# Recurrent attention and a squared-ReLU layer on one core: other load shapes, v through GpSimd's casting queue, state by head pairs, and priorities written out

## The chip, the cores and the metric

The kernel runs on one core of one Trainium2 chip. The metric is the device time of one execution in microseconds, as the median of several runs. Engines are called by the names that the profile uses: PE (TensorE matmuls), PEld (TensorE weight loads), DVE (VectorE), ACT (ScalarE), POOL (GpSimd), SP (SyncE, which issues most DMAs).

## The reference

Inputs are r, k and v of shape (4, 8, 768, 48), that is 4 batches, 8 heads, 768 steps and 48 columns, w and u of shape (8, 48), and two weight matrices of 384 x 2048 and 2048 x 384, all float32.

```python
for t in range(S):
    kt, vt, rt = (k[:, :, t].copy(), v[:, :, t].copy(), r[:, :, t].copy())
    cur = np.einsum('bhd,bhe->bhde', u[None] * kt, vt)
    y[:, :, t] = np.einsum('bhd,bhde->bhe', rt, state + cur)
    state = w[None, :, :, None] * state + np.einsum('bhd,bhe->bhde', kt, vt)
...
h = x @ w_in                 # x: y with the heads of a token side by side, (3072, 384)
r = np.maximum(h, 0.0)
return (r * r @ w_out).astype(np.float32)
```

## The kernel before

**Units.** The 768 steps are cut into 6 chunks of 128. A unit is one chunk of one batch, all heads: 24 units, unit i being chunk i // 4 of batch i % 4. In a unit the recurrence becomes matmuls. r is multiplied by w to the power (t - 64) (`wpos`) and k by w to the power (63 - t) (`wneg`), both by `scale` on DVE (L321), into a padded bfloat16 tile `rkw`. It is transposed to `rkT`, for units 0 to 5 by PE (`turn` L341, evicted by ACT, L345), and from unit 6 on by a DMA (`turn_dma` L330). Then come `at` (L358, r times k for all pairs of steps), `mask` (DVE, L370), `rk` (DVE, L350) and `sums` (L378 for the u term, L383 for the unit's part of the state), `diag_v` (`dv`, DVE, L392), `y_mm` (L421, and L427 with the state of the chunk before), and `evict_y` (`yb`, DVE, L436). The state is kept in float32 as (128, 4, 48): partitions 0 to 63 hold the even head of a pair and 64 to 127 the odd one. `state_add` (L400, L402) and `state_cast` (L412) therefore run twice, on 64 partitions each, and `state_decay` (L406) once. v is loaded as float32 and cast by ACT (`cast_v`, L325).

**The layer.** `yb` is transposed into `xT`, for units 0 to 5 by PE (L452, evicted by ACT, L456) and later by a DMA (L445). `mm1` (L468) makes a block of 512 columns of h in one PSUM bank: 12 matmuls for one unit, or 6 with both units of a pair (units 8 to 19 go in pairs). ACT applies ReLU (L476), and the square is made by ACT (L483) or DVE (L485) after the pattern `SQUARES`. `mm2` (L492) accumulates 16 matmuls a unit in quarters of four, ACT evicts (L499), and SP stores. The last unit is stored in two parts (L508 to L520).

**Weights.** The two matrices come in four pieces each, `w_in_q0` to `w_in_q3` and `w_out_q0` to `w_out_q3`, cast to bfloat16 by GpSimd's DMA queue. Each piece is held back by a small copy (L306) that reads one load of the table `FRONT`, so that it is issued only when that load has landed.

**Order.** Nothing is scheduled at run time. `Plan.run` takes all steps with an engine, a cost, what they need, the buffers and banks they take, and a rank. It plays them through in time: each engine takes the first step by rank that is ready, and PE is given matmuls on a constant tile (`fill`, L276) while it would be idle in the first 16 us. The instructions are then written out per engine in that order, and each engine works through its own list strictly in order, waiting where an operand is not there. A DMA in the plan has a cost on its queue and a transfer of its own; SP's transfers pass in the order of issue.

**Start.** `wrow` (L222) is w broadcast to 128 partitions by one DMA on ACT's queue. ACT takes its logarithm (`lnw`, L241) and the two exponentials `wpos` and `wneg` (L245). `wu` (w and u again) comes by GpSimd's queue, is transposed by PE (L281), copied by DVE (L284), and makes `uwb` (POOL, L287 and L290) and `wend`, w to the power 128 (ACT, L293 and L294).

Of the kernel before, what the change touches and what calls it, by code (L numbers as in the profile page):

```python
# [16 lines left out]
class Plan:  # L17
# [9 lines left out]
    def __init__(self, lags, cold, spare):  # L27
        self.lags = lags
        self.cold = cold
        self.spare = spare  # L30
        self.steps = []
        self.at = {}
        self.users = {}
        self.place = {}

    def add(self, key, engine, cost, emit, needs=(), rank=0.0, new=(), uses=(), move=None):
        s = dict(key=key, engine=engine, cost=cost, emit=emit, rank=rank, new=new, move=move)
        s["needs"] = [n for n in needs if n is not None]
        self.at[key] = s
        self.steps.append(s)  # L40
        for x in tuple(new) + tuple(uses):
            self.users.setdefault(x, []).append(s)

    def run(self, room, banks, count):
# [10 lines left out]
        begin, until, tight, loose = self.spare  # L55
        held[0] = "spare"
# [7 lines left out]
        def ready(s, e):  # L64
            if s["move"]:
                return s["end"] + moved
# [96 lines left out]
def kernel(  # L163
# [23 lines left out]
    NPAD = 5  # L187
    SQUARES = 'AMAMAAAM'
    FRONT = (
        ("I", 0, ("kt", 1)), ("I", 1, ("kt", 3)), ("I", 2, ("kt", 3)), ("O", 0, ("kt", 3)),  # L190
        ("I", 3, ("kt", 3)), ("O", 1, ("kt", 3)), ("O", 2, ("kt", 3)), ("O", 3, ("kt", 3)),
# [5 lines left out]
    loads = ctx.enter_context(tc.tile_pool(name="loads", bufs=6))  # L197
# [6 lines left out]
    plan = Plan((0.9, 0.0, 0.2, 0.33, 0.12), (5.5, 1.9), (1.25, 16.0, 0.057, 0.08))  # L204
# [16 lines left out]
    wrow = const.tile([128, dm], F32)  # L221
    nc.scalar.dma_start(out=wrow, in_=w.rearrange("h d -> (h d)").unsqueeze(0).to_broadcast([128, dm]))  # L222
    nc.scalar.preload_act_table_set("natural_log_exp_and_others")
    warm = const.tile([128, 128], BF16)
    nc.vector.memset(warm, 1.0)  # L225
    wu = const.tile([HP, 2, 2, 64], F32)
# [3 lines left out]
    nc.gpsimd.dma_start(out=wu[:, 1, :, :D], in_=u.rearrange("(p o) d -> p o d", o=2))  # L230

    iota_i = const.tile([128, 1], mybir.dt.int32)
    nc.gpsimd.iota(iota_i, pattern=[[0, 1]], base=0, channel_multiplier=1)
    up = const.tile([128, 1], F32)
    nc.vector.tensor_scalar(up, iota_i, 1.0, -float(C // 2), ALU.mult, ALU.add)
    down = const.tile([128, 1], F32)
    nc.vector.tensor_scalar(down, iota_i, -1.0, float(C // 2 - 1), ALU.mult, ALU.add)
    ident4 = const.tile([HP, HP], F32)
    make_identity(nc, ident4)
    lnw = const.tile([128, dm], F32)  # L240
    nc.scalar.activation(lnw, wrow, AF.Ln)  # L241
    wpos = const.tile([128, H, D], F32)
    wneg = const.tile([128, H, D], F32)
    for wx, by in ((wpos, up), (wneg, down)):
        nc.scalar.activation(wx.rearrange("p h d -> p (h d)"), lnw, AF.Exp, scale=by)  # L245
# [15 lines left out]
    st32 = [const.tile([128, HP, D], F32, name=f"st32_{b}") for b in range(B)]  # L261
    stb = [const.tile([128, HP, 2 * D], BF16, name=f"stb_{b}") for b in range(B)]
    for b in range(B):
        nc.vector.memset(stb[b], 0.0)

    wend_c = const.tile([128, HP], F32)
    wend = wend_c.unsqueeze(2).to_broadcast([128, HP, D])
# [7 lines left out]
    def fill():  # L275
        nc.tensor.matmul(out=banks[0][:, :128], lhsT=warm, rhs=warm, start=True, stop=True)  # L276

# [17 lines left out]

    def load(i, name):
        c, b = units[i]
        src = {"rt": r, "kt": k, "vt": v}[name]
        x = loads.tile([C, H, D], F32, name=name)
        nc.sync.dma_start(  # L300
            out=x, in_=src[b, :, c * C : (c + 1) * C, :].rearrange("h s d -> s h d")
        )
# [14 lines left out]
    def scale(i, x):  # L317
        t = tiles[i]
        t["rkw"] = rkw_b[i % NPAD]
        src, wx = (t["kt"], wneg) if x else (t["rt"], wpos)  # L320
        nc.vector.tensor_tensor(t["rkw"][:, x, :, :, :D], pair(src), pair(wx), ALU.mult)  # L321

    def cast_v(i):
        tiles[i]["vb"] = work.tile([C, H, D], BF16, name="vb")
        nc.scalar.copy(tiles[i]["vb"], tiles[i]["vt"])  # L325

    def turn_dma(i):
        t = tiles[i]
        t["rkT"] = work.tile([128, 2, HP, C], BF16, name="rkT")
# [5 lines left out]
    def turn(i, x):  # L335
        t = tiles[i]
        t["tp", x] = bank("h", i, "rk", x).bitcast(BF16)[:, : HP * C].rearrange("p (a c) -> p a c", a=HP)
        if x == 0:
            t["rkT"] = work.tile([128, 2, HP, C], BF16, name="rkT")
# [3 lines left out]
    def evict_rk(i, x):  # L343
        t = tiles[i]
        nc.scalar.copy(t["rkT"][:, x], t["tp", x])  # L345
# [48 lines left out]
    def state_add(i):  # L394
        c, b = units[i]
        for o in range(2):
            sl = slice(o * 64, o * 64 + 64)
            x = tiles[i]["s"][sl, :, o * D : (o + 1) * D]
            if c == 0:
                nc.vector.tensor_tensor(st32[b][sl], x, wend[sl], ALU.mult)  # L400
            else:
                nc.vector.tensor_tensor(st32[b][sl], x, st32[b][sl], ALU.add)  # L402
# [5 lines left out]
    def state_cast(i):  # L408
        b = units[i][1]
        for o in range(2):  # L410
            sl = slice(o * 64, o * 64 + 64)
            nc.scalar.copy(stb[b][sl, :, o * D : (o + 1) * D], st32[b][sl])  # L412
# [127 lines left out]

    add("w", ACT, 3.9, None, rank=-1e3)
    add("wk", ACT, 0.48, None, rank=-1e3, needs=["w"])
    copy("begin", SP, 0.74, None, rank=-1e3)
    add("wu", POOL, 4.6, None, rank=-1e3)
# [3 lines left out]
    add("wend", ACT, 0.4, end_columns, rank=10, needs=["copied"])  # L548
    for n, (what, q, gated) in enumerate(FRONT):
        copy(  # L550
            (what, q), POOL, 1.0, do(weights, gated, q, what), rank=n,
            move=((2.35, 98, 1.25, 0.0) if what == "I" else (2.05, 78, 1.25, 0.0)), needs=[gated], uses=[gated],
        )
    for i in range(NU):
# [4 lines left out]
        for n, name in enumerate(("rt", "kt", "vt")):  # L559
            copy(  # L560
                (name, i), SP, 0.55, do(load, i, name), rank=rank + 0.1 * n, move=(1.06, 16, 0.67, 1.0),
                new=[(name, i)],
            )
        for x in range(2):
            add(
                ("scale", i, x), DVE, 0.47, do(scale, i, x), rank=a - 4 + 0.1 * x,
                needs=[("rt", i) if x == 0 else ("kt", i), "wk" if x else "w", ("scale", i - 1, x) if i else None],
                new=[("rkw", i)] if x == 0 else (), uses=[(("rt", "kt")[x], i), ("rkw", i)],
            )
        add(  # L570
            ("vb", i), ACT, 0.405, do(cast_v, i), rank=a + 0.5, needs=[("vt", i), ("rkT", i) if i < 24 else ("scale", i, 1)],
# [142 lines left out]
```

## Time and profile before

| | |
|---|---|
| median of 3 runs | 178.01 us (177.97 to 179.85) |
| the profiled execution | 179.7 us, of which the span from the first to the last instruction 177.9 |
| PE busy | 167.5 us (94%), 2080 matmuls |
| DVE, ACT busy | 128.7 and 128.8 us (72% each) |
| POOL busy | 11.4 us (6%) |
| DMA | 29.05 MB in 107,385 packets, 101,985 of them under 512 bytes |
| granted clock | 1.0 |

The page shows one execution. The busy shares say which engine was occupied, not which one the others waited for; that is told by the waits and by the chain that ended last. The slices are 177.9 / 40 = 4.45 us each, one digit being tenths of a slice. "Packets" are runs of contiguous bytes: a load of r, k or v for one unit is 192 KB in 1,024 runs of 192 bytes (48 float32 of one head and step). A line such as `L402 ... x32 | 11.3, 352 | 0.2` reads: 32 instructions, 11.3 us busy, 352 ns each, 0.2 us of idle time of that engine just before them.

### The profile page before, as it was taken

The page shows a single profiled execution, that of the slowest core. Times are in us where ns is not written, and L with a number is a line of the kernel's source. Part 1 is how long each engine was busy: PE and PEld are TensorE (multiplying, and loading weights), DVE is VectorE, ACT ScalarE, POOL GpSimd, SP SyncE. Part 2 cuts the span into 40 slices and gives each one's busy share as a digit, 9 for nine tenths or more (in the row PEclk, how much of TensorE's full clock was granted, in tenths as well). Part 3 has the DMA queues.
Part 4 walks back from the last instruction along what each step waited for, and adds up shares of the span by engine and source line. Part 5 has one row for each costly group of instructions (what it writes and reads, how often), then busy time and mean ns, then how long its engine had stood idle before and what let it go on. Part 6 is the DMA issues. An engine that isn't in the chain of part 4 may idle for free.

```text
span 177.9 us, 5106 instructions
## 1 busy us (share of the span) xinstructions
PE 167.5 (94%) x2080; PEld 135.2 (76%) x2080; DVE 128.7 (72%) x279; ACT 128.8 (72%) x268; POOL 11.4 (6%) x35
## 2 busy tenths in 40 slices
PE   7699689999999999989979999899999999999993
PEld 7599479977786886876776796786795797878762
DVE  3389996565989899769779698589598695853100
ACT  2738889999385985597488599488597499659820
POOL 7120950000000000000000000000000000000000
PEclk9999999999999999999999999999999999999999
DMA  5999999999797888869879889999998897940212
GB/s 103 192 179 181 163 197 197 208 190 179 93 208 128 169 155 171 175 132 206 174 161 185 176 166 191 133 201 185 163 199 172 187 201 135 314 135 0 71 67 90
DMA packets 107385, 29.05 MB, mean 163 GB/s; under 512 B 101985, under 2 KB 106849, under 8 KB 107361
## 3 DMA queue, kind: packets, MB, share of 16 engines
q1 hardware_dynamic: 104976, 25.37, 75.1%
q0 software_dynamic: 2240, 3.15, 10.0%
q8 instruction: 16, 0.26, 0.6%
q10 hardware_dynamic: 144, 0.20, 0.6%
q14 instruction: 9, 0.07, 0.1%
HBM read 20.65 MB, written 4.72 MB: 143 GB/s over the span
## 4 chain that ended last, share of the span: by engine, by line
PE 57%; DMA 18%; DVE 17%; issue 3%; ACT 2%; SPq 1%; ACTq 0%
PE bank L492 22%; PE bank L468 22%; DMA rkT<-rkw 8%; DMA rt<-in_r_dram 5%; DVE am L370 4%; DVE rkw L321 4%; DVE yb L436 3%; PE bank L358 3%; DMA xT<-yb 2%; PE bank L276 2%; DMA wrow<-in_w_dram 2%; DVE dv L392 2%; DVE g L485 2%; PE bank L421 1%; PE bank L508 1%
## 5 line engine op out<-in xcount | busy, mean ns | idle before, releaser
L468 PE MATMUL bank<-xT,w_in_q 128*128 128x128 bf16 (+1 forms) x864 | 71.8, 237 | 0.5 <-ACT xT L456 0.3
L476 ACT ACTIVATE gr<-bank 128x512 f32<-128x512 f32 x96 | 55.0, 601 | 19.5 <-PE bank L468 18.9
L468 PEld LDWEIGHTS <-w_in_q 128*128 128x128 bf16 x864 | 64.4, 114 | 3.3 <-issue 0.7
L492 PE MATMUL bank<-w_out_q,g 128*128 128x384 bf16 x368 | 65.1, 326 | 0.0
L492 PEld LDWEIGHTS <-g 128*128 128x128 bf16 x368 | 34.4, 98 | 20.0
L370 DVE TENSOR_TENSOR am<-bank,smask 128x512 bf16<-128x512 f32 x48 | 31.8, 684 | 8.2 <-PE bank L358 8.1
L483 ACT ACTIVATE g<-gr 128x512 bf16<-128x512 f32 x60 | 37.3, 639 | 0.6
L485 DVE TENSOR_TENSOR g<-gr 128x512 bf16<-128x512 f32 x36 | 24.6, 687 | 13.1 <-ACT gr L476 13.0
L499 ACT COPY osb<-bank 128x384 f32<-128x384 f32 x23 | 11.0, 484 | 10.1 <-PE bank L492 7.9
L412 ACT CAST stb<-st 64x192 bf16<-64x192 f32 x40 | 14.0, 350 | 5.1 <-DVE st L406 4.4
L350 DVE TENSOR_TENSOR rk<-rkT 128x512 bf16<-128x512 bf16 x24 | 10.1, 422 | 7.7 <-DMA rkT<-rkw 5.6
L321 DVE TENSOR_TENSOR rkw<-rt,wpos 128x384 bf16<-128x384 f32 x24 | 13.2, 552 | 2.5 <-DMA rt<-in_r_dram 1.7
L436 DVE TENSOR_TENSOR yb<-bank,dv 128x384 bf16<-128x384 f32 x24 | 13.3, 555 | 2.3 <-PE bank L427 1.7
L392 DVE TENSOR_TENSOR dv<-vb,bank 128x384 f32<-128x384 bf16 x24 | 13.1, 545 | 2.6 <-PE bank L383 2.6
L321 DVE TENSOR_TENSOR rkw<-kt,wneg 128x384 bf16<-128x384 f32 x24 | 13.2, 551 | 0.6 <-DMA kt<-in_k_dram 0.3
L276 PE MATMUL bank<-warm 128*128 128x128 bf16 x108 | 11.9, 275 | 1.1 <-DVE warm L225 1.1
L358 PE MATMUL bank<-rkT 64*128 64x128 bf16 x192 | 9.8, 222 | 2.8 <-DMA rkT<-rkw 1.9
L325 ACT CAST vb<-vt 128x384 bf16<-128x384 f32 x24 | 12.2, 508 | 0.2
L402 DVE TENSOR_TENSOR st<-bank,st 64x192 f32<-64x192 f32 x32 | 11.3, 352 | 0.2
L358 PEld LDWEIGHTS <-rkT 64*128 64x128 bf16 x192 | 5.5, 96 | 7.5 <-issue 2.9
L276 PEld LDWEIGHTS <-warm 128*128 128x128 bf16 x108 | 9.6, 128 | 1.4 <-DVE warm L225 1.1
L345 ACT COPY rkT<-bank 128x512 bf16<-128x512 bf16 x12 | 6.9, 585 | 4.5 <-PE bank L341 4.5
(54 smaller groups left out, 97.8 us busy)
## 6 DMA issues: line engine op xcount, KB each, us to landing
rt<-in_r_dram SPq DMA_DIRECT2D x24, 192.0 KB, 4.2
kt<-in_k_dram SPq DMA_DIRECT2D x24, 192.0 KB, 4.0
vt<-in_v_dram SPq DMA_DIRECT2D x24, 192.0 KB, 4.4
out_dram<-osb SPq DMA_DIRECT2D x23, 192.0 KB, 2.8
w_in_q<-in_moe_w_in_dram POOLq DMA_DIRECT2D x4, 384.0 KB, 7.2
w_out_q<-in_moe_w_out_dram POOLq DMA_DIRECT2D x4, 384.0 KB, 13.1
rkT<-rkw SPq DMA_TRANSPOSE x18, 3.8
xT<-yb SPq DMA_TRANSPOSE x18, 3.0
```

The source lines that it names most:

```text
L276: nc.tensor.matmul(out=banks[0][:, :128], lhsT=warm, rhs=warm, start=True, stop=True)
L321: nc.vector.tensor_tensor(t["rkw"][:, x, :, :, :D], pair(src), pair(wx), ALU.mult)
L358: nc.tensor.matmul(out=t["at"][o][:, p, :], lhsT=t["rkT"][sl, 1, p, :], rhs=t["rkT"][sl, 0, p, :], start=True, stop=True,)
L370: nc.vector.tensor_tensor(am, t["at"][o], smask.unsqueeze(1).to_broadcast([C, HP, C]), ALU.mult)
L392: nc.vector.tensor_tensor(t["dv"], t["vb"], t["d"].unsqueeze(2).to_broadcast([C, H, D]), ALU.mult)
L412: nc.scalar.copy(stb[b][sl, :, o * D : (o + 1) * D], st32[b][sl])
L436: nc.vector.tensor_tensor(t["yb"], t["y"], t["dv"].rearrange("p h d -> p (h d)"), ALU.add)
L468: nc.tensor.matmul(out=t["h", s][:, a], lhsT=turned, rhs=chunks[c]["xT"][:, n, b : b + m, :], start=(n == 0), stop=(n == NK - 1),)
L476: nc.scalar.activation(t["gr", s], t["h", s], AF.Relu)
L483: nc.scalar.activation(g, x, AF.Square)
L485: nc.vector.tensor_tensor(g, x, x, ALU.mult)
L492: nc.tensor.matmul(out=t["o"], lhsT=chunks[units[i][0]]["g"][:, f, units[i][1], :], rhs=w_out_q[f // 4][:, f % 4, :], start=(f == 0), stop ...
```

## The change

1. w is loaded as one row on one partition. ACT takes the logarithm there, and PE spreads it: `spread_log` by four float32 matmuls with a row of ones, 32 partitions for each pair of heads, and `spread_all` by one to all 128. `power_r` (four exponentials), `power_k` and `power_rest` make `wpos`, `wneg` and `wnat`.
2. r of units 0 to 5 is loaded with a pair of heads and 32 groups of four steps on the partitions, so that one run is four steps, 768 bytes; two DMAs for one. `scale` reads it in that layout, the transposes take one step of each group of four, and `evict_rk` puts the columns back in order as it copies. From unit 6 on r is loaded as before and multiplied by `wnat`.
3. v of units 6 to 23 is loaded by GpSimd's queue, cast to bfloat16 on the way, into 8 buffers of their own (`load_v`). They stand last in GpSimd's list, after all weights, and no `cast_v` is left for them. For the plan each of them needs kt of the unit before; as an instruction it waits for its buffer alone.
4. The state is (128, 4, 96): both heads of a pair in all partitions, with a zero in `wend` for the cross terms. `state_add` and `state_cast` are one instruction each.
5. A table `TURNS` gives single steps a rank of their own; `FRONT` gates w_in_q1 by kt of unit 2 (it was unit 3), w_in_q2 by vt of unit 1, and the pieces of w_out and w_in_q3 by kt3, kt4, rt4 and vt4; `SQUARES` gives six of eight squares to ACT, not five; `rkw` has 8 buffers for 5, loads 7 for 6, `rkT` and `vb` 6 for 4; some costs in the plan are others.

On PE's list the fillers go from 108 to 87. On DVE's list yb of unit 0 stands behind the scaling of r of unit 2, the masks of unit 5 behind the scaling of k of unit 7, and yb of unit 5 behind rk of unit 6. SP's list begins rt0, kt0, rt1, vt0, kt1, kt2, vt1, vt2, rt2, rt3, kt3, kt4, vt3, rt4, vt4, rt5, rt6, vt5, kt5, kt6, rt7, kt7, rt8, and then the first transpose, rkT of unit 6. GpSimd's list has w_in_q0, w_in_q1, `wend`, w_in_q2, w_out_q0, w_out_q1, w_in_q3, w_out_q2, w_out_q3, and then the 18 loads of v.

```diff
     def add(self, key, engine, cost, emit, needs=(), rank=0.0, new=(), uses=(), move=None):
+        kind, which = (key[0], key[1] if len(key) == 2 else key[1:]) if isinstance(key, tuple) else ("", key)
+        rank = self.turns.get(kind, {}).get(which, rank)
...
-    NPAD = 5
-    SQUARES = 'AMAMAAAM'
+    NPAD = 8
+    NVB = 8
+    SQUARES = 'AAAMAAAM'
+    TURNS = {
+        "rt": {
+            0: -42.651, 1: -34.809, 11: 17.689, 12: 18.622, 14: 29.051, 16: 41.802, 18: 45.897, 2: -17.657, 21:
...
-        ("I", 0, ("kt", 1)), ("I", 1, ("kt", 3)), ("I", 2, ("kt", 3)), ("O", 0, ("kt", 3)),
-        ("I", 3, ("kt", 3)), ("O", 1, ("kt", 3)), ("O", 2, ("kt", 3)), ("O", 3, ("kt", 3)),
+        ("I", 0, ("kt", 1)), ("I", 1, ("kt", 2)), ("I", 2, ("vt", 1)), ("O", 0, ("kt", 3)),
+        ("O", 1, ("kt", 4)), ("O", 2, ("rt", 4)), ("O", 3, ("vt", 4)), ("I", 3, ("kt", 4)),
...
-    wrow = const.tile([128, dm], F32)
-    nc.scalar.dma_start(out=wrow, in_=w.rearrange("h d -> (h d)").unsqueeze(0).to_broadcast([128, dm]))
+    wrow = const.tile([1, dm], F32)
+    nc.scalar.dma_start(out=wrow, in_=w.rearrange("h d -> (h d)").unsqueeze(0))
...
+    def spread_log():
+        spread["r"] = bank("h", "rlog")[:, : 2 * D]
+        for a in range(HP):
+            sl = slice(a * 32, a * 32 + 32)
+            nc.tensor.matmul(
+                out=spread["r"][sl], lhsT=ones[:, :32], rhs=lnw[:, a * 2 * D : (a + 1) * 2 * D], start=True, stop=True,
+            )
+
+    def spread_all():
+        spread["k"] = bank("h", "klog")[:, :dm]
+        nc.tensor.matmul(out=spread["k"], lhsT=ones, rhs=lnw, start=True, stop=True)
+
+    def power_r():
+        for l in range(4):
+            nc.scalar.activation(wpos[:, l].rearrange("p o d -> p (o d)"), spread["r"], AF.Exp, scale=up[:, l : l + 1])
...
-        nc.sync.dma_start(
-            out=x, in_=src[b, :, c * C : (c + 1) * C, :].rearrange("h s d -> s h d")
-        )
+        if name == "rt" and i < NPE:
+            src = src.rearrange("(a o) (q l) d -> o a q (l d)", o=2, l=4)
+            for o in range(2):
+                nc.sync.dma_start(out=x[:, o * 4 : o * 4 + 4, :].rearrange("p l d -> p (l d)"), in_=src[o])
+        else:
+            nc.sync.dma_start(out=x, in_=src.rearrange("h s d -> s h d"))
...
+    def load_v(i):
+        c, b = units[i]
+        tiles[i]["vb"] = work.tile([C, H, D], BF16, name="vc", bufs=NVB)
+        nc.gpsimd.dma_start(out=tiles[i]["vb"], in_=v[b, :, c * C : (c + 1) * C, :].rearrange("h s d -> s h d"))
...
+            turned = t["tp", 0].rearrange("p l (a q) -> p a l q", a=HP)
+            nc.scalar.copy(t["rkT"][:, 0].rearrange("p a (q l) -> p a l q", l=4), turned)
...
-        for o in range(2):
-            sl = slice(o * 64, o * 64 + 64)
-            x = tiles[i]["s"][sl, :, o * D : (o + 1) * D]
-            if c == 0:
-                nc.vector.tensor_tensor(st32[b][sl], x, wend[sl], ALU.mult)
-            else:
-                nc.vector.tensor_tensor(st32[b][sl], x, st32[b][sl], ALU.add)
+        nc.vector.tensor_tensor(st32[b], tiles[i]["s"], st32[b] if c else wend, ALU.add if c else ALU.mult)
...
+        else:
+            copy(("vb", i), POOL, 1.1, do(load_v, i), rank=a + 50, needs=[("kt", i - 1)], move=(1.06, 16, 1.4, 0.0, LATE[0]), new=[("vc", i)])
```

## The prediction

> **What bounds the kernel now.** I read the busy shares by slice first, then sums over stretches, then the waits of TensorE, then the DMA queues.
>
> ```profile
> PE   7699689999999999989979999899999999999993
> DVE  3389996565989899769779698589598695853100
> ...
> PEclk9999999999999999999999999999999999999999
> DMA  5999999999797888869879889999998897940212
> ```
>
> TensorE (PE) is full from slice 6 (27 us) on, at the full granted clock; the DMA engines are at nine tenths over the first ten slices already. The sums over stretches put numbers to it (us; PE, PEld, DVE, ACT, POOL busy; clock; DMA share; GB/s):
>
> ```profile
> 0.00:10.00 10.00, 7.48 (x69) 6.75 (x69) 4.13 (x22) 4.92 (x9) 3.95 (x20) 1.00 0.89 153
> 10.00:20.00 10.00, 9.21 (x161) 8.26 (x156) 9.37 (x20) 6.56 (x14) 2.75 (x5) 1.00 1.09 180
> 20.00:30.00 10.00, 8.67 (x157) 7.60 (x155) 8.93 (x20) 9.31 (x20) 4.68 (x11) 1.00 1.13 183
> ...
> 60.00:80.00 20.00, 19.60 (x251) 15.51 (x248) 16.45 (x34) 15.38 (x34) 0.00 (x0) 1.00 0.81 159
> 80.00:100.00 20.00, 18.83 (x194) 14.07 (x194) 16.29 (x37) 13.84 (x30) 0.00 (x0) 1.00 0.87 174
> 100.00:120.00 20.00, 19.07 (x218) 16.21 (x216) 17.14 (x36) 15.58 (x33) 0.00 (x0) 1.00 0.98 179
> 120.00:140.00 20.00, 19.63 (x201) 14.56 (x199) 16.41 (x36) 13.93 (x31) 0.00 (x0) 1.00 0.99 177
> ```
>
> Of the first 30 us PE is idle for 2.5 + 0.8 + 1.3 = 4.6, and 11.9 of its busy time there is the filler of L276. So 16.5 us at the front do no work, and from 60 to 140 only 0.4 + 1.2 + 0.9 + 0.4 = 2.9 are idle. What the change can win lies in these two sums: up to 16.5 at the front, up to 2.9 later. The later waits of PE are for transposes by DMA:
>
> ```profile
> PE bank L358 <- DMA rkT<-rkw: 1.9, 2, 1.0
> PE bank L421 <- DVE am L370: 0.6, 1, 0.6
> PE bank L468 <- DMA xT<-yb: 0.3, 1, 0.3
> ```
>
> Why the front is slow: the first product with w_in_q0 starts at 16.8, but w_in_q1 is issued at 18.5 and lands at 24.7 (its landing takes 6.2), and PE is dense from 25.0. Meanwhile DVE is full (9.4 of 10) with the masks, state and products of units 0 to 3. The weights also block the loads. This is rt of unit 5, issued at 19.2:
>
> ```profile
> L300 SPq DMA_DIRECT2D rt<-in_r_dram x1: 784/784/784, 19.2 to 19.2; - x1
> DMA to landing us min/median/max: 14.8/14.8/14.8
> ...
> ```
>
> Alone a load lands 1.05 after the one before (rt, kt of unit 0 at 5.35 and 6.35). This one has 1,024 runs, 64 for each of 16 engines; from 24.7 until it lands at 34.0 w_in_q2, w_out_q0, w_in_q3 and most of w_out_q1 pass, 24 + 8 + 24 + 6 = 62 runs an engine. So the two queues take turns run by run: a 192 byte run of SP for each 2 or 6 KB run of GpSimd.
>
> ```profile
> q1 hardware_dynamic: 104976, 25.37, 75.1%
> q0 software_dynamic: 2240, 3.15, 10.0%
> ...
> q10 hardware_dynamic: 144, 0.20, 0.6%
> ```
>
> The weights are 10.0% of 177.9 = 17.8 us of all engines, 127 ns a run, against 20 ns on SP's queue.
>
> **The change, part by part.**
>
> *w as one row.* Its 128 broadcast runs (q10, 0.6%, 1.1 us) become one. It landed at 4.4; now the table load (until 2.46) is what the logarithm waits for: 2.5 + 0.5 = 3.0. New are four float32 matmuls of 96 columns, one of 384 and four exponentials in place of one. Float32 rows before: 4x4 at 0.26 (L281). For 96 columns I bound by 0.04 (four of L427, bf16, take 0.17) and 0.4, and take 0.25, so 1.0 for four, behind 22 fillers that end at 3.5; exponentials of 96 columns between 0.2 (128x4, L293) and 0.35 (64x192, L412), taken 0.3, four 1.2. wpos is ready at about 5.9, against 5.57: 0.3 later (bounds 0.6 earlier, 0.7 later). So the first product does not come forward; only the 1.1 us of DMA is won.
>
> *r of units 0 to 5 in 768 byte runs.* 256 runs for 1,024. The weights read 6.3 MB in 17.8 us, 354 GB/s; at that rate 192 KB take 0.55; the upper bound is the old 1.05. I take 0.6: six times 0.45 = 2.7 us of DMA. The two issues for one cost SP 0.4 more, hidden since SP is ahead. Transposing by four interleaved rows and the strided eviction keep size and count (0.58, L345), at most twice that, on ACT, which is idle 3.4 of 10 us there.
>
> *Order of weights.* w_in_q0 to q2 are gated by kt1, kt2 and vt1, not kt1, kt3, kt3. With 1.05 and 0.6 per load, landings are rt0 4.3, kt0 5.3, rt1 5.9, vt0 7.0, kt1 8.0, kt2 9.1, vt1 10.1, vt2 11.2, rt2 12.0. Before, kt1 landed at 9.5 and the first weight runs moved 2.8 later; now they move from 10.8, three pieces without a gap, and by turns w_in_q0 lands at 14.7 (was 16.4), q1 at 17.3 (24.7), q2 at 20.2 (27.5). kt3, starved, lands at 20.4 (was 17.9) and gates w_out_q0, at 26 (29.6); w_in_q3 at 31 (32.0). Walking DVE's new order with its rows (scale 0.47 a step, rk 0.34, mask 0.6, dv, state and yb 0.47), yb of units 0, 1, 2, 3 ends at 14.0, 16.0, 19.5, 26.2; before at 14.0, 18.1, 22.3, 26.5. The first L468 block is then at 15.3, and PE has done 11 blocks of L468 and 4 of L492 by 31.5, against 10.6 and 1: 0.4 x 0.67 + 3 x 0.65 = 2.2, and about 0.9 more of small matmuls. Lead at 31.5: **3.1 us**.
>
> *v of units 6 on through GpSimd's queue.* 18 loads leave SP's queue, and ACT loses 18 casts (0.51). GpSimd issues them after its last weights with no wait but for 8 buffers, so eight run beside SP's loads from 34 on (from 23, four pieces of w_out at 2.0 and w_in_q3 at 2.4, with SP's turns between). GpSimd issues 384 runs in 0.77 and 128 in 0.56: 1,024 runs about 1.3, hidden, as it has nothing else. Who pays is unit 6. rkT of unit 6 lands after: weights 17.8, six r 3.6, twelve k and v 12.6, five r and k 5.3, itself 1.6: 40.9, from 2.6 on 43.5, plus 3.1 of latency as the same count misses before (46.1 counted, 49.2 seen): 46.6 with no v ahead, 54 with seven and a half (7.9). Taking turns, almost all get ahead, but then the gaps are filled: 51; with only the four that the plan foresees, 48. I take 49.5. DVE holds yb of unit 5 behind rk of unit 6, so unit 5's L468 starts near 52, while PE is out of other work at about 49. PE waits 2.6; before, it lost 1.3 from 31 to 60. Lead at 60: 3.1 - 2.6 + 1.3 = **1.8** (bounds -3 and 4.4).
>
> *Later.* SP issued six DMAs a unit (0.6 + 0.7 + 1.0 + 1.3 + 1.2 + 0.6 = 5.4 by their medians) in the 6.4 us that a unit takes (60 to 174.8, 18 units); now five, 4.4. rkT rings are 6 deep for 4, pads 8 for 5, loads 7 for 6. Of the 2.9 idle I give back half, **1.4** (bounds 0 and 2.9).
>
> *State by pairs, squares.*
>
> ```profile
> L402 DVE TENSOR_TENSOR st<-bank,st 64x192 f32<-64x192 f32 x32 | 11.3, 352 | 0.2
> L392 DVE TENSOR_TENSOR dv<-vb,bank 128x384 f32<-128x384 bf16 x24 | 13.1, 545 | 2.6 <-PE bank L383 2.6
> L412 ACT CAST stb<-st 64x192 bf16<-64x192 f32 x40 | 14.0, 350 | 5.1 <-DVE st L406 4.4
> ```
>
> Two adds of 0.35 become one of 0.55 (20 units, -3), the decay goes from 0.35 to 0.55 (16, +3), two casts of 0.35 become one of 0.48 (20, -4.3 on ACT). Squares go from five ACT of eight to six: 12 of 0.64 to ACT, 12 of 0.69 off DVE. ACT -9.2 - 4.3 + 7.7 = -6, DVE -8. I price that at nothing after 30 us: PE covers both at 72%. If PE's cover went, it would be gain, not loss.
>
> The profiled execution took 179.7 with a span of 177.9; the median is 178.0, so the sum is made on the span. 177.9 - 1.8 - 1.4 = 174.7, in terms of the median **174.8**.
>
> **Rivals.**
>
> *Nothing gets in unit 6's way* (v's runs write half the bytes and are cheap, rkT at 46.6): lead 4.4 at 60 and all of 2.9: 170.7. For: GpSimd's runs cost by bytes, 127 ns for 2 to 6 KB. Against: the DMA share is 1.1 there, so something must wait.
>
> *v's runs are dear* (slower). Place: eight v beside kt5 to rkT6, from 34 on. If one takes 1.6 us, not 1.05, then 7.5 x 2.65 = 20 us pass until rkT of unit 6, which lands at 55; PE waits 8 at 49, the lead at 60 is -3.6, and ten more v add 5.5 us to DMA shares of 0.87 to 0.99, so the 2.9 stays: 181.5. It decides from 1.35 us a load. For: no row shows small casting runs. Against: SP's runs of the same source size take 1.05 a load.
>
> *v passes as one block.* If GpSimd's queue keeps its turn for many small runs, kt5 comes at 44 (34.3 + 8 x 1.05 + 1) rather than 39.6 (34.3 + 2.5 loads x 2.1), masks of unit 5 wait for kt7 at 50, rkT at 52: lead -0.2, later 1.4: 176.8. The Trainium skill ("DMA: Bandwidth & Descriptors", Queues, rings and completion order) says that an engine drains a whole packet, some 9 to 17 descriptors, from one ring before it switches; by that rule this rival is what happens. The trace of before has SP's 192 byte runs going one at a turn, and no small runs on GpSimd's queue.
>
> *The priorities do not do what they say*: with one more late load ahead of DVE's order the gain is gone, 178.
>
> **How the numbers follow.** The forecast (172 to 177.5) has 0.42, of it 0.34 faster by over 1% (under 176.2), 0.08 within 1%, which is about what a measurement can tell from no change. Cheap v 0.22, all faster. Dear v 0.20 (0.19 slower, 0.01 same). Block 0.10 (0.03, 0.06, 0.01). Priorities 0.06 (0.01, 0.02, 0.03). Sums: 0.60, 0.17, 0.23. The range, 169.5 to 181.5, takes in both prices of v.
>
> **What would show it.** Right: w_in_q1 landing near 17, dense PE from 17 to 19, PE waiting 2 to 3 us near 50 for unit 5 or 6, less than 2 us idle from 60 to 140. Wrong: a PE wait over 4 us near 28 (vt4 late) or 50, v loads landing over 1.35 us apart, or first scaling past 6.5.

## The result, and the profile after

The changed kernel takes 188.33 us (median of 4 runs, 187.38 to 188.96) against 178.42 us (177.97 to 179.85) for the kernel before: ratio 1.0537, 95% interval 1.0458 to 1.0615. It is slower by 5.4%; 174.8 us, 1.8% faster, was predicted, and the range ended at 181.5. The profiled execution took 188.17 us with a span of 186.0, 8.1 more than the 177.9 of before. All ratios below are to the kernel before, run beside the others on the same chip, and compare undisturbed executions alone; `r_192_v_gated` had three of those (175.1 to 175.8 us) in ten, the others at 178.5 to 182.6, so its ratio is the least certain.

The slices of the changed kernel (4.65 us each; before, PE was full from slice 6 on and the clock was 9 everywhere):

```profile
PE   7598749646999999999999999999999999999993
DVE  3369264614729998995898795999677467261200
...
PEclk9999978996999999999999999999999999999999
DMA  2699959999998999999999999999963973023012
```

Counted from 0, PE has two stretches of holes, slices 4 and 5 and slices 7 to 9, and is full only from slice 10 (46.5 us). DMA starts at 2 and 6 tenths where it started at 5 and 9. The sums by stretch (us; PE, PEld, DVE, ACT, POOL busy; clock; DMA share; GB/s):

```profile
0.00:10.00 10.00, 6.76 (x50) 4.74 (x51) 3.95 (x31) 5.38 (x10) 3.69 (x18) 1.00 0.52 116
10.00:20.00 10.00, 9.25 (x158) 8.10 (x156) 8.47 (x17) 6.87 (x13) 4.12 (x11) 1.00 1.06 184
20.00:30.00 10.00, 6.34 (x84) 6.03 (x82) 3.58 (x7) 5.84 (x12) 3.10 (x8) 0.83 0.73 137
30.00:40.00 10.00, 7.87 (x115) 5.84 (x114) 5.75 (x11) 10.00 (x20) 4.24 (x7) 1.00 1.12 203
40.00:60.00 20.00, 16.60 (x211) 13.95 (x212) 10.51 (x20) 12.80 (x24) 3.50 (x5) 0.91 1.49 131
60.00:80.00 20.00, 20.00 (x309) 15.81 (x308) 19.41 (x41) 14.22 (x28) 3.16 (x4) 1.00 1.29 150
...
120.00:140.00 20.00, 20.00 (x216) 16.22 (x215) 16.79 (x34) 13.21 (x27) 0.00 (x0) 1.00 0.95 182
```

Up to 60 us PE is idle for 3.2 + 0.8 + 3.7 + 2.1 + 3.4 = 13.2 us; before it was 2.5 + 0.8 + 1.3 + 0 + 0 = 4.6. From 60 to 140 it is not idle at all, where it was for 2.9. That makes 8.6 - 2.9 = 5.7 of the 8.1. PE's busy sum makes 2.2 (169.6 for 167.5, with 2.8 us less of fillers), part of it at the lower clock of 0.83 and 0.91. So the whole loss lies in the first 60 us.

The waits (who, for whom: total us, times, longest):

```profile
DVE rkw L460 <- DMA rt<-in_r_dram: 11.9, 4, 4.7
...
PE bank L485 <- DVE rkw L460: 6.7, 3, 4.1
```

L460 is the scaling of r of units 0 to 5, L485 the transposes. DVE waits 11.9 us for r, and PE waits 6.7 behind it; neither stood in the waits of before at more than 2.1. Three pieces of the chain that ended last (start, us, what):

```profile
13.37 6.80 SPq L437
20.21 3.70 SPq L437
...
27.75 14.94 DMA rt<-in_r_dram
```

SP stands 10.5 us on two issues (kt of unit 4, vt of unit 3), and half of r of unit 5, issued at 27.75, is there at 42.7. Its scaling starts at 42.8, before at 37.4. The rows of the page that belong to the parts of the change:

```profile
q1 hardware_dynamic: 81600, 21.83, 64.4%
q0 software_dynamic: 20960, 4.92, 29.2%
...
L465 POOL DMA_DIRECT2D vc<-in_v_dram x18 | 15.8, 891 | 66.8 <-PE bank L567 24.8
...
L493 ACT COPY rkT<-bank 128x512 bf16<-128x512 bf16 x6 | 7.9, 1314 | 4.8 <-PE bank L485 4.8
```

q0 went from 17.8 to 54.3 us of all engines (29.2% of 186.0); the strided eviction L493 takes 1.31 us where the plain one took 0.58.

### The profile page after: what moved, and what is told of

Its sections match the earlier page's. It is cut to its first block, busy times and chain, and to the rows that moved or that the text cites. A ratio compares the mean times of both kernels' runs of the same rounds, so it can differ in the third digit from the quotient of the medians.

```text
span 186.0 us, 5068 instructions
## 1 busy us (share of the span) xinstructions
PE 169.6 (91%) x2069; PEld 135.9 (73%) x2069; DVE 120.4 (65%) x256; ACT 128.5 (69%) x246; POOL 27.4 (15%) x56
## 3 DMA queue, kind: packets, MB, share of 16 engines
q0 software_dynamic: 20960, 4.92, 29.2%
## 4 chain that ended last, share of the span: by engine, by line
PE 75%; SPq 14%; DMA 8%; issue 1%; DVE 0%; DVEq 0%
PE bank L608 31%; PE bank L632 31%; SPq L437 9%; DMA rt<-in_r_dram 8%; SPq L435 5%; PE bank L506 3%; PE bank L561 2%; PE bank L567 2%; PE bank L531 2%; PE bank L648 1%; PE bank L526 1%; PE bank L485 0%; DVE rkw L460 0%; PE bank L592 0%; DVE osb L660 0%
## 5 line engine op out<-in xcount | busy, mean ns | idle before, releaser
L616 ACT ACTIVATE gr<-bank 128x512 f32<-128x512 f32 x96 | 55.0, 604 | 11.1 <-PE bank L608 10.3
L623 ACT ACTIVATE g<-gr 128x512 bf16<-128x512 f32 x72 | 44.7, 646 | 0.8
L518 DVE TENSOR_TENSOR am<-bank,smask 128x512 bf16<-128x512 f32 x48 | 31.5, 683 | 5.9 <-PE bank L506 5.7
L625 DVE TENSOR_TENSOR g<-gr 128x512 bf16<-128x512 f32 x24 | 16.4, 688 | 17.7 <-ACT gr L616 17.7
L465 POOL DMA_DIRECT2D vc<-in_v_dram x18 | 15.8, 891 | 66.8 <-PE bank L567 24.8
L552 ACT CAST stb<-st 128x384 bf16<-128x384 f32 x20 | 10.4, 520 | 19.8 <-DVE st L548 9.1
L576 DVE TENSOR_TENSOR yb<-bank,dv 128x384 bf16<-128x384 f32 x24 | 13.2, 552 | 6.0 <-PE bank L567 5.3
L485 PE MATMUL bank<-identb,rkw 128*128 128x128 bf16 x48 | 5.7, 265 | 6.7 <-DVE rkw L460 6.7
L561 PEld LDWEIGHTS <-am 128*128 128x128 bf16 x192 | 8.2, 98 | 4.1 <-DVE am L518 2.5
L493 ACT COPY rkT<-bank 128x512 bf16<-128x512 bf16 x6 | 7.9, 1314 | 4.8 <-PE bank L485 4.8
L460 DVE TENSOR_TENSOR rkw<-rt,wpos 128x384 bf16<-128x384 f32 x6 | 3.3, 556 | 11.9 <-DMA rt<-in_r_dram 11.9
L540 DVE TENSOR_TENSOR dv<-vc,bank 128x384 f32<-128x384 bf16 x18 | 9.7, 545 | 2.0 <-PE bank L526 1.4
L381 PE MATMUL bank<-warm 128*128 128x128 bf16 x87 | 9.1, 265 | 1.1 <-DVE warm L323 1.1
L457 DVE TENSOR_TENSOR rkw<-rt,wnat 128x384 bf16<-128x384 f32 x18 | 9.9, 549 | 0.2 <-DMA rt<-in_r_dram 0.2
```

The costliest lines, as they stand in the source:

```text
L465: nc.gpsimd.dma_start(out=tiles[i]["vb"], in_=v[b, :, c * C : (c + 1) * C, :].rearrange("h s d -> s h d"))
L518: nc.vector.tensor_tensor(am, t["at"][o], smask.unsqueeze(1).to_broadcast([C, HP, C]), ALU.mult)
L561: nc.tensor.matmul(out=y[:, 2 * p + o, :], lhsT=t[f"am{o}"][:, p, :], rhs=t["vb"][:, 2 * p + o, :], start=(o == 0 and p == 0), stop=c == 0 ...
L576: nc.vector.tensor_tensor(t["yb"], t["y"], t["dv"].rearrange("p h d -> p (h d)"), ALU.add)
L616: nc.scalar.activation(t["gr", s], t["h", s], AF.Relu)
L623: nc.scalar.activation(g, x, AF.Square)
```

## Experiments

**First: r itself.** Theories: the halves of r are slow in themselves (T1); three early pieces of w_in starve the loads whatever r looks like (T2); the strided eviction is on the path (T3); SP's issues wait for earlier landings, so that two loads for one take places (T4); v stands in the way (T5); the written ranks lose (T6). `r_192` undoes the layout of r and keeps everything else, with every engine's order:

```diff
-        if name == "rt" and i < NPE:
-            src = src.rearrange("(a o) (q l) d -> o a q (l d)", o=2, l=4)
-            for o in range(2):
-                nc.sync.dma_start(out=x[:, o * 4 : o * 4 + 4, :].rearrange("p l d -> p (l d)"), in_=src[o])
-        else:
-            nc.sync.dma_start(out=x, in_=src.rearrange("h s d -> s h d"))
+        nc.sync.dma_start(out=x, in_=src.rearrange("h s d -> s h d"))
...
```

(with one power of w for all r, and the plain eviction)

> The changed kernel with one part undone: r of units 0 to 5 is loaded in 192 byte runs by one DMA, as before the change, multiplied by wnat and evicted without reordering; every engine keeps the order of the changed kernel. Theory 1 (each half of r runs on 4 of the 16 DMA engines, because the slowest dimension of its source has size 4): r of units 2, 3 and 5 lands 2 to 8 us earlier, the waits of DVE for r (11.9 us) fall under 4, and the time goes from 188.3 to 176 to 181. Theory 2 (three pieces of w_in without a gap starve whatever SP loads behind them): 192 byte runs are 64 an engine instead of 32 on four engines, so r of unit 3 lands no earlier than 22, and the time stays between 185 and 189. Theory 3 (the eviction with strides, 1.31 us instead of 0.58, is on the path): the time falls by at most six times 0.7 = 4.4, to 184.

Measured: 180.05 us, ratio 1.0104 (1.0037 to 1.0172). So the layout of r, that is the two loads of each r, the powers and the eviction that go with it, costs 8.3 of the 9.9 us, and T2 is left with little.

Two layouts keep the 768 byte runs and put another dimension outside. `r_768_by_pairs` takes four loads a unit, one for each pair of heads, with 32 groups of steps outermost. `r_768_by_steps` keeps two loads and puts the step groups outside the pairs; the powers of w are spread to match. The cuts show the loads alone.

```diff
 # r_768_by_pairs
+            src = src.rearrange("(a o) (q l) d -> a q o (l d)", o=2, l=4)
+            for a in range(HP):
+                nc.sync.dma_start(out=x[a * 32 : a * 32 + 32].rearrange("p (o l) d -> p o (l d)", o=2), in_=src[a])
...
 # r_768_by_steps
-            src = src.rearrange("(a o) (q l) d -> o a q (l d)", o=2, l=4)
+            src = src.rearrange("(a o) (q l) d -> o q a (l d)", o=2, l=4)
...
```

> The changed kernel, where only the loads of r of units 0 to 5 are cut otherwise: four DMAs, one for each pair of heads, 32 partitions and 64 runs of 768 bytes each, so that the slowest dimension is 32 on both sides; layout, eviction and order stay. Theory 1: all 16 engines serve each of them, the sixteenth increments of its semaphore show (a landing can be told in the profile), r waits of DVE fall from 11.9 to under 4, and the time is 176 to 182, with SP issuing four DMAs of about 0.5 for two. Theory 2: no change beyond 2 us, 186 to 190. Theory 3: no change, since the eviction is the same.

> The changed kernel with the 128 partitions of r of units 0 to 5 in another order, groups of four steps outside and pairs of heads inside, so that the slowest dimension of the source is 32 and not 4; still two DMAs of 768 byte runs. The spread of w for it takes four float32 matmuls to all 128 partitions, which makes the first powers some 1 us later. Theory 1: r on 16 engines, time 175 to 181, the first scaling at about 6.2 instead of 5.6. Theory 2: 186 to 190. Theory 3: as in the changed kernel, 188.

Measured: 183.30 us, ratio 1.0209 (1.0103 to 1.0315), and 184.35 us, ratio 1.0361 (1.0282 to 1.044). Both gain over 1.0537 with the same bytes in the same runs; what differs is which dimension is outermost in a load: T1. Neither is as fast as was expected under T1 (176 to 182 and 175 to 181). `r_768_by_steps` stays behind `r_192`, which has four times as many runs; for `r_768_by_pairs` the intervals overlap. T1 can also be seen in the changed kernel's trace: the semaphore of each half of r is counted up five times, once soon after the issue and four times at the landing (the first half at 1.84, then at 4.18, 4.19, 4.40 and 4.48), that of a load with 32 or more outermost sixteen times.

`evict_order` reads the bank in strides and writes side by side:

```diff
-            turned = t["tp", 0].rearrange("p l (a q) -> p a l q", a=HP)
-            nc.scalar.copy(t["rkT"][:, 0].rearrange("p a (q l) -> p a l q", l=4), turned)
+            turned = t["tp", 0].rearrange("p l (a q) -> p a q l", a=HP)
+            nc.scalar.copy(t["rkT"][:, 0].rearrange("p a (q l) -> p a q l", l=4), turned)
```

> The changed kernel with only the eviction of r's transposes walked in another order: it reads PSUM with a stride and writes SBUF contiguously, the same elements to the same places. Theory 3: if the write's stride is what costs, the instruction goes from 1.31 to about 0.6 and the time falls by up to 4 us. Theory 1 and 2: the time stays at 187 to 189, since what DVE and PE wait for is the load of r.

Measured: 187.57 us, ratio 1.0494 (1.0396 to 1.0592), not to be told from the changed kernel. The eviction itself is cured, as its row shows:

```profile
L493 ACT COPY rkT<-bank 128x512 bf16<-128x512 bf16 x6 | 3.5, 587 | 6.5 <-PE bank L485 6.5
```

It takes 0.59 us for 1.31, 4.4 us less in six, and ACT waits longer for the transposes (6.5 us for 4.8); the time hardly follows. T3 falls as the cause.

**Second: two loads or one; v; ranks.** `r_768_one_dma` is `r_768_by_steps` with both halves in one load of 256 runs:

```diff
-            for o in range(2):
-                nc.sync.dma_start(out=x[:, o * 4 : o * 4 + 4, :].rearrange("p l d -> p (l d)"), in_=src[o])
+            nc.sync.dma_start(
+                out=x.rearrange("p (o l) d -> p o (l d)", o=2), in_=src.rearrange("h (q l) d -> q h (l d)", l=4)
+            )
...
```

> As r_768_by_steps (groups of four steps outside, so all 16 engines), but r of a unit comes by one DMA of 256 runs in place of two. Theory 4: SP lets only eight DMAs be in flight, each issue waits for the eighth before it, and halves of r fill these places with little data, so that SP's queue runs dry (DMA share 0.83 and 0.47 at 20 to 24 us against 1.14 and 1.17 with 192 byte runs) and r of unit 4 comes in two pieces 3 us apart. Then one DMA brings the time from 184.4 to 178 to 181, and the queue stays busy at 20 to 24. Rival (the powers that come 1 us later and the strided eviction make the difference to 180.0): 183 to 185.

Measured: 178.88 us, ratio 1.0088 (1.0041 to 1.0135). One load for two is worth 1.0361 - 1.0088 = 2.7%, 4.9 us, with the same bytes, runs and engines. That more loads cost time fits T4, its mechanism doesn't. SP takes eight semaphores in turn, and where an issue stood for long, the load that had the same semaphore eight issues before had landed: vt of unit 5, in the kernel before, stood 7.9 us on its issue from 22.0, and the eighth load before it was there at 17.1; r of unit 5, in `r_768_one_dma`, 9.4 us from 14.5, the eighth before it at 10.1. What the two traces do show is that each issue takes SP some 0.6 us, so with two loads for each r what follows is issued later. This is kt of unit 3 in `r_768_by_steps`, then in `r_768_one_dma`:

```profile
L441 SPq DMA_DIRECT2D kt<-in_k_dram x1: 592/592/592, 10.6 to 10.6; - x1
...
DMA to landing us min/median/max: 10.9/10.9/10.9
```

```profile
L441 SPq DMA_DIRECT2D kt<-in_k_dram x1: 601/601/601, 8.6 to 8.6; - x1
...
DMA to landing us min/median/max: 3.8/3.8/3.8
```

w_in_q0 and w_in_q1 are issued at 9.4 and 10.3 in both. Issued behind them, kt of unit 3 lands at 21.5, ahead of them at 12.4; it gates w_out_q0, which is issued at 22.0 instead of 13.4, and r of unit 5 lands at 35.5 instead of 29.9. This fits the 4.9 us but isn't shown to be all of it: the clock of `r_768_by_steps` also fell to 0.70 from 30 to 40 us (1.00 in the other). And the number of loads alone doesn't order the runs: `r_768_by_pairs` has four and is not behind `r_768_by_steps` (the powers of w that fit it are spread as in the change, in 0.5 us of matmuls, those of `r_768_by_steps` in 2.0). The two kernels in the first microsecond of their r (DMA busy in 40 slices of 25 ns from 2.2 to 3.2 us, and the rate); the changed kernel first, then `r_768_one_dma`:

```profile
DMA  7009000090000060000000012022228031221232
GB/s 31 31 31 61 31 31 31 0 31 0 0 0 31 31 31 0 0 0 0 0 0 0 0 2 62 0 63 62 62 62 92 0 92 31 61 61 31 92 61 92
```

```profile
DMA  0129249070916105112594465899999999998999
GB/s 0 31 92 123 61 92 123 0 92 31 92 61 31 61 31 61 61 61 31 31 246 92 154 215 184 276 338 276 307 430 338 307 307 492 307 353 292 446 323 315
```

From 2.8 us on both move r alone. With the pairs outermost the 768 byte runs keep some two tenths of the engines busy, as four of sixteen would, at some 60 GB/s; with the step groups outermost nine tenths, at 276 to 492 GB/s.

`r_192_v_gated` and `r_768_one_v_gated` add one line to those two kernels, so that v of a unit starts only when k of the unit before has landed:

```diff
     def load_v(i):
+        nc.gpsimd.tensor_copy(gate, tiles[i - 1]["kt"][:, 0, :1])
```

> As r_192 (r as before the change), and each load of v by GpSimd is held back by a small copy that reads k of the unit before it, which is what the plan assumes and the instruction does not wait for. Theory 5: the eight loads of v that GpSimd issues at 27 to 35 us take turns with k of units 5 to 8 and the first transpose; held back, k of unit 5 is scaled at 37 to 39 instead of 42.9, yb of unit 5 comes at 48 to 50 instead of 53.3, and the time goes from 180.0 to 176 to 178.5. Rival (the order of DVE and PE is what loses, not v): 179.5 to 181.

> r in 768 byte runs by one DMA on all engines, and v held back by k of the unit before. If theories 4 and 5 both hold, this is the best so far, 174.5 to 178; if only 4 holds, 178 to 181; if neither, 183 to 185.

Measured: ratio 0.9893 (0.9836 to 0.995) for `r_192_v_gated`, against 1.0104 without the gate; and 178.73 us, ratio 1.008 (1.0039 to 1.0121), for `r_768_one_v_gated`, no gain over 1.0088. So the two disagree on T5, and the gain of `r_192_v_gated` rests on three executions: the median of all ten is 180.56 us, no gain over the 180.05 of `r_192`.

`r_192_no_turns` is `r_192` with `TURNS` empty:

```diff
-    TURNS = { ... }
+    TURNS = {}
```

> As r_192, but with the table of single priorities empty, so that the plan takes the plain ranks again, with the same gates for the weights. Theory 6 (the written priorities put DVE's work behind late loads, such as the masks of unit 5 behind k of unit 7): the time falls from 180.0 to 177 to 179. Rival (they are worth something, and what loses lies in the loads): 182 to 187.

Measured: 181.16 us, ratio 1.015 (1.0029 to 1.0271), against 1.0104 with the ranks. The ranks do not lose (T6 falls as a cause); that they win is not shown.

**Third: parts alone.** `r_768_one_contig` joins the two mends, one load and the eviction written side by side. The other three put one part of the change each into the kernel before. The cuts show lines that come in, not those that they replace.

```diff
 # r_768_one_contig: r_768_one_dma and
+            turned = t["tp", 0].rearrange("p l (q a) -> p a q l", a=HP)
+            nc.scalar.copy(t["rkT"][:, 0].rearrange("p a (q l) -> p a q l", l=4), turned)
 # state_by_pairs_alone: the kernel before and
+        nc.vector.tensor_tensor(st32[b], tiles[i]["s"], st32[b] if c else wend, ALU.add if c else ALU.mult)
...
+        nc.scalar.copy(stb[b], st32[b])
...
 # v_cast_alone: the kernel before and
+            copy(("vb", i), POOL, 1.1, do(load_v, i), rank=a + 50, needs=[("kt", i - 1)], ...)
 # weights_early_alone: the kernel before and
+        ("I", 0, ("kt", 1)), ("I", 1, ("kt", 2)), ("I", 2, ("vt", 1)), ("O", 0, ("kt", 3)),
+        ("O", 1, ("kt", 4)), ("O", 2, ("rt", 4)), ("O", 3, ("vt", 4)), ("I", 3, ("kt", 4)),
```

> r of units 0 to 5 in one DMA of 256 runs, as in r_768_one_dma, and in addition the eviction of turned r reads its bank in strides and writes side by side, as in evict_order, where that eviction took 0.587 us on average and not 1.31. If the strided write lies mostly beside other work, as evict_order said (0.8 us below the changed kernel), this is 0.5 to 1 us below r_768_one_dma: 178.1 (177.4 to 178.9). If with the loads mended the eviction is what the front waits for next (six times 0.73 us, 4.4 us), it is 175.5 (174.5 to 176.5), below the kernel before.

> The kernel before with one part of the change: the state by head pairs (one addition, one decay and one cast of 384 columns where there were two of 192, one, and two), the planner's costs left as they are so that the order stays. By the rows, ACT loses 40 x 0.35 us and gains 20 x 0.52 us (3.6 us less), DVE stays within 1 us. If the state is off the path, as the prediction priced it, it is the kernel before within 0.9 us: 177.7 (176.8 to 178.6). If the missing waits past 60 us of the changed kernel come from the shorter chain of the state, some 2.5 us of waits go: 175.2 (174.5 to 176.2).

> The kernel before with one part of the change: v of units 6 on through GpSimd's casting queue, planned anew with the costs of the changed kernel for these loads. If that queue's records, 29 to 30 ns for 96 bytes against 15 to 18 ns for SP's 192 byte runs, hold up the loads around 40 to 60 us, v is what the mended kernels still lose in front: 180 (178.6 to 182). If the prediction's reading holds, that the work it takes from SP and ACT removes waits past 60 us, it is 176.3 (175.0 to 177.4).

> The kernel before with one part of the change: the order of the eight weights and the loads that they wait for (three pieces of w_in early, then the pieces of w_out, the last piece of w_in at the end). If three pieces one after the other starve the loads of units 2 to 5 (theory T2), it is 180 (178.7 to 182), with unit 5's k landing past 40. If earlier weights bring blocks of the first multiplication forward without harm, as the prediction had it, it is 176 (174.8 to 177.2).

Measured: `r_768_one_contig` ratio 1.0023 (0.9978 to 1.0068), the kernel before; `state_by_pairs_alone` 1.001 (0.9977 to 1.0044), nothing; `v_cast_alone` 183.63 us, 1.0249 (1.0204 to 1.0294); `weights_early_alone` 182.52 us, 1.0186 (1.0145 to 1.0227). Both of the last lose alone, though the whole change with r mended does not. Either other parts of the change make up for them, or the order that the planner makes anew for them is what costs; these runs don't separate the two. What is common to the kernels here with v on GpSimd's queue is a slower transposing load. The answers on the tile rkT say how long those issued between 38 and 75 us took to land, in the kernel before, in `r_768_one_contig`, and in `contig_v_gated` (told below); for the last two the landing of the first such load isn't among them:

```profile
DMA to landing us min/median/max: 3.2/3.7/4.8
```

```profile
DMA to landing us min/median/max: 4.7/5.3/6.3
```

```profile
DMA to landing us min/median/max: 3.7/4.3/6.9
```

The first of them takes 4.8 us before (44.4 to 49.2), 7.8 in `v_cast_alone` (47.1 to 54.9), 8.8 in `r_768_one_contig`, where it is in the chain that ended last (42.3 to 51.1), and 4.1 in `contig_v_gated` (41.8 to 45.9).

**Fourth: the rest of the gain.** From `r_768_one_contig`: `v_after_turned` lets v of units 7 on wait for the turned r and k of the unit before, `v_on_sp` gives v back to SP and ACT, `weights_as_before` takes the old table `FRONT`; all three were planned anew. `contig_v_gated` adds the one line of the gated runs above and keeps every order.

```diff
 # v_after_turned
+        if i > NPE:
+            nc.gpsimd.tensor_copy(gate, tiles[i - 1]["rkT"][:, 0, 0, :1])
 # v_on_sp
-        for n, name in enumerate(("rt", "kt", "vt") if i < NPE else ("rt", "kt")):
+        for n, name in enumerate(("rt", "kt", "vt")):
...
 # weights_as_before
...
+        ("I", 0, ("kt", 1)), ("I", 1, ("kt", 3)), ("I", 2, ("kt", 3)), ("O", 0, ("kt", 3)),
+        ("I", 3, ("kt", 3)), ("O", 1, ("kt", 3)), ("O", 2, ("kt", 3)), ("O", 3, ("kt", 3)),
```

> r_768_one_contig, with each v of units 7 on held in GpSimd's queue until the unit before has its turned r and k, and planned for that. In r_768_one_contig the transposing transfer of unit 6 takes 8.8 us (42.3 to 51.1) beside v of units 6 on, where it takes 4.8 us in the kernel before; if the v loads beside it are what the mended kernel still loses in front, it lands by 48 and the time is 2 to 3 us below r_768_one_contig, which measured 1.0023 of the kernel before: ratio 0.985 to 0.995, 176 to 178 us. If the transfer is slow for another reason, or a v that is asked for this late is waited for, the ratio is 1.00 to 1.02.

> r_768_one_contig with v of units 6 on loaded by SP and cast by ACT, as in the kernel before, and planned anew. If v through GpSimd's queue costs more in front than it gives later (v_cast_alone: ratio 1.025), this is faster than r_768_one_contig: ratio to the kernel before 0.98 to 0.995. If that run's loss came from its order of work alone, and the searched order of the change is made for v on GpSimd, the waits past 60 us come back here: ratio 1.01 to 1.03.

> r_768_one_contig with the order of the weights, and the loads that they wait for, as in the kernel before. If the early pieces cost what they did alone (weights_early_alone: ratio 1.019), the ratio to the kernel before falls to 0.98 to 0.99 and first multiplications begin no later than 17. If the searched order of the change needs its weights early, TensorE waits for w_in near 20 to 26 and the ratio is 1.005 to 1.03.

> r_768_one_contig with a copy on GpSimd, ahead of each v load of units 6 on, that reads k of the unit before, so that a v starts only when that k has landed; every order as in the change. In r_768_one_contig the transposing transfers of units 6 on land 4.7 to 6.3 us after their issue, in the kernel before 3.2 to 4.8, with the same gate in r_768_one_v_gated 3.5 to 6.8, and TensorE idles 2.1 us near 47 to 51 for the work of units 5 and 6. If v beside them is what keeps r_768_one_contig at the time of the kernel before, these 2 us go: ratio 0.985 to 0.995. If it is hidden work, as r_768_one_v_gated said (no gain), the ratio stays at 1.00 (0.997 to 1.008).

Measured: `v_after_turned` 1.0184 (1.0128 to 1.024), `v_on_sp` 1.0344 (1.0295 to 1.0394), `weights_as_before` 1.0299 (1.0257 to 1.034), `contig_v_gated` 177.69 us, 0.9957 (0.9913 to 1.0001). Taking v or the weights out of the change loses too. So each of the two loses when put in alone and when taken out alone; their price can't be read apart from the order that goes with them. The gate under an unchanged order shortened the transposing loads (4.3 for 5.3) and brought the ratio from 1.0023 to 0.9957, with intervals that overlap. `contig_v_gated` is the best version with a firm number, and it is not shown to beat the kernel before by 1%.

## Why the prediction was wrong, by its own steps

**r in 768 byte runs: the step that failed.** The sum gave a unit 0.6 us, from the rate of the weights on all engines, with the old 1.05 as the upper bound, so a loss was excluded. In the changed kernel the 256 runs of unit 0 stretch from 2.2 to 5.2 us (3.0) and those of unit 5, beside weights and v, from 34.2 to 42.2 (8.0). The rate of the weights was one of all engines; here the outermost dimension of each half is the four pairs of heads, and four engines carry it. The run length was weighed, the outermost dimension wasn't looked at. In `r_768_one_dma`, spread wide, 256 runs take 1.2 us (2.25 to 3.43): even there 0.6 was too little, though not by much (units 1 to 3 took 1.2, 1.1 and 0.9). DVE's 11.9 us of waits for r are what followed, and undoing the layout gave back 8.3 of the 9.9 us.

The Trainium skill ("DMA: Bandwidth & Descriptors", Why a DMA increments its semaphore by 16 and not by 1) says it: the number of engines is the largest one up to 16 that divides the slowest dimension of both sides. For a half, with 4 outermost, that is 4; for `r_768_by_steps`, with 32 and 128, 16. The traces agree: two tenths busy against nine. This rule spoke against the change and was missing from the prediction.

**"The two issues for one cost SP 0.4 more, hidden since SP is ahead": also failed.** An issue takes SP some 0.6 us when nothing holds it, and it isn't hidden: with two loads for each r, kt of unit 3 was issued behind the first weights (`r_768_by_steps`, above). An issue can also stand much longer: 6.80 and 3.70 us in the changed kernel. What holds it there is open. In the kernel before, SP's issues that ended between 4.2 and 12.3 us did so when 2,050 to 2,300 of its runs, two loads' worth, were still to move; that an issue lasts until the queue has drained so far is one reading, and no run tried it. Scaling of k of unit 5 starts at 50.8 in the changed kernel, 46.6 in `r_768_by_steps`, 42.9 in `r_192`, 41.6 in `r_768_one_dma` and 39.8 before, and the times of these five stand in the same order, the third and the fourth with intervals that overlap.

**The order of the weights: half right.** With r as before (`r_192`) w_in_q0 to q2 land at 14.9, 18.1 and 20.6 and w_out_q0 at 24.6; 14.7, 17.3, 20.2 and 26 were predicted. In the changed kernel they land at 18.3, 21.2, 24.1 and 32.6. But the lead that was to come of it is smaller. By 31.5 us `r_192` has done 120 matmuls of w_in and 13 of w_out, before 127 and 4, 10 x 0.67 + 3.25 x 0.65 = 8.8 us of work for 7.8: 1.0, not 2.2. Right after it PE waits 3.2 us (to 35.35) for r of unit 5, which is scaled at 34.7; before, its list had other blocks ahead until 37.4. So the lead of 3.1 is gone even with r mended. The sum to 60 us was also wrong by itself: its term of +1.3, "before, it lost 1.3 from 31 to 60", stands in no row. Before, PE was busy for 10.00 of 10 us from 30 to 40 and 20.00 of 20 from 40 to 60; the 1.3 lies between 20 and 30. Without it the lead at 60 is 0.5 and the forecast 176.1.

**w as one row: right.** The last power was ready at 5.15 (5.9 predicted), each 0.34 (0.3); r of unit 0 then came last.

**Strided eviction: size wrong, place right.** It took 1.31, over twice 0.58; but cured alone it changed nothing that can be measured, and with r mended 1.0088 became 1.0023, intervals overlapping.

**v: price right for the rival, effect not.** v of units 6 to 13 lands 2.0 us apart (44.65 to 58.87), past the 1.35 from which the rival "v's runs are dear" was to decide. Yet the loss sits ahead of v. The gate, which takes v out of the way, is worth 0.7% in the mended kernel (at most 1.6% by the ends of the two intervals, and not clear of nothing), and under the order of the change v belongs to the best version. The rival "v passes as one block" did not happen: in `r_192` v of units 6 to 10 lands at 36.6, 38.9, 40.5, 42.7 and 44.5, with a load of SP's between each two.

**Later: sized too small.** All 2.9 us of waits past 60 are gone, not 1.4, in the changed kernel and in the mended one (PE busy 40.00 of 40.00 in both stretches):

```profile
40.00:60.00 20.00, 18.36 (x244) 13.68 (x243) 14.55 (x31) 12.19 (x24) 1.75 (x2) 1.00 1.54 154
60.00:100.00 40.00, 40.00 (x484) 31.30 (x483) 35.08 (x70) 27.92 (x55) 5.25 (x6) 1.00 1.38 175
100.00:140.00 40.00, 40.00 (x440) 32.61 (x439) 31.57 (x63) 30.61 (x61) 1.75 (x2) 1.00 0.99 177
```

That is `r_768_one_contig`: span 176.2, 1.7 less than the profiled execution of before. Up to 60 us its PE is idle for 5.7 against 4.6, so 1.1 of the 2.9 is given back; 1.6 of the 5.7 lie between 40 and 60, where v and the transposing loads meet and PE was not idle before. The profiled execution of before was itself 1.7 us above its median, and over the runs compared the two kernels are the same (1.0023); how much of the 2.9 a usual execution of before has was not traced.

**State by pairs priced at nothing: right** (1.001). The squares were not tried alone.

**The signs named.** "First scaling past 6.5" did not come (5.6). "A PE wait over 4 us" came, 4.1 us from 39.3, for r of unit 5 and not for vt4 or v; so did loads of v that land over 1.35 apart. Of the signs that it is right, only "less than 2 us idle from 60 to 140" came; w_in_q1 landed at 21.2 and not near 17. That the change doesn't do what it says was held against the ranks; it was true of the load of r.

What stays open is what v and the early weights cost by themselves, since every kernel that took one of them in or out was planned anew, whether the gate on v helps `r_192` (1.0104 to 0.9893, on three executions) when it doesn't help `r_768_one_dma`, and what holds a long issue on SP.

## What to carry to other kernels

For each load that is rearranged, look at the outermost dimension on both sides before the length of the runs: runs four times as long, but on a quarter of the engines, came with a loss of 5%, and undoing that layout gave back 8.3 of 9.9 us. Count the issues when a load is split to get a layout: each took its engine some 0.6 us and put off what is issued behind it, and joining two halves gave back 4.9 us. In a kernel with a searched order, a part planned anew brings a new order with it, so test a part with every engine's order kept, as the gate and the layouts of r were.

## What the hardware showed

- A load whose outermost dimension is 4 moved some 60 GB/s alone; the same runs with 32 outermost 276 to 492.
- The casting queue's 1,024 runs a unit (96 bytes written) land 2.0 us apart beside SP's loads, and GpSimd's issue takes 0.89 us, less than the 1.3 estimated. Beside them the transposing loads take 5.3 us for 3.7.
- ACT's copy of 128x512 bfloat16 out of a bank takes 1.31 us when each element is written 8 bytes from the last, 0.59 when it is read in strides and written side by side.
- A float32 matmul with one row of ones stands as two instructions in the rows: for 384 columns 2 x 0.92, 1.6 us busy.
- The granted clock fell to 0.83 (20 to 30 us) and 0.91 (40 to 60) in the changed kernel around waits of 2.4 and 4.1 us. It is not the length of one wait alone: `v_cast_alone` shows 0.83 from 20 to 30 with no gap of PE over 0.75 us there.
